# The first chunk's inverse deviations by ScalarE and VectorE instead of GpSimd, fewer warm-up matmuls, and another order of the queues

## The chip, the core and the metric

The kernel runs on one core of a Trainium2 chip. The metric is the device time of one execution in microseconds (us), as the median of several runs. The engines are TensorE (PE; its weight loads are listed as PEld), VectorE (DVE), ScalarE (ACT), GpSimd (POOL) and SyncE (SP), which here only issues transfers.

## The reference, cut to what matters

```
def _layernorm(x, axis=-1, eps=1e-5):
    return (x - mean) / jnp.sqrt(var + eps)

h  = x + A(_layernorm(x))       # x: 2048 rows of 448, bf16
h2 = h + B(_layernorm(h))
```

A is attention with 16 heads of 28: each position attends to 8 keys, at distances 0, 2, ..., 14 behind it, then the output projection wo. B is a mixer: LayerNorm, w1, gelu, a shift of four column groups along the sequence, w2, residual, then LayerNorm, w3 (448 to 1792), gelu, w4 and another residual.

## The kernel before, in words

The 2048 rows are worked in four chunks c = 0 to 3 of four 128-row tiles. For the tail the MLP regroups the tiles into five groups g = 0 to 4 (2, 4, 4, 4 and 2 tiles). Every operation is recorded once with a tag, in the functions of `_fast_path`. The tags that the text uses are:

- A1_c: statistics (`ln_stats`, L547), inverse deviation (`inv_std`, L551), normalised rows `lntm` (`normalize`, L562), and their transpose into `hT`, by TensorE and a copy out of PSUM for chunks 0 and 1, by a DMA transpose for 2 and 3
- V_c, QK_c: the projections (`phase_V` L639, `phase_QK` L685); each output is copied out of PSUM by ScalarE or VectorE (tags .e0 to .e3). `pad_wqk` (L631) spreads the weights beforehand
- S_c.g, E_c.g, AV_c.g, N_c.g: scores on TensorE, exp on ScalarE and multiplication by the mask on VectorE, values on TensorE, and the division by the softmax's sum, for half g of the heads (`phase_att`, L701). For chunks 0 and 1 the division is done block by block on VectorE (`norm_blocks`, L751). For chunks 2 and 3 the output is copied to `osb` (O), the sums travel through DRAM (Zg, Z: `zp`, `rzp`, `rz_scratch`, `rzb`; `norm_dma`, L765), and VectorE multiplies (N)
- WO_c (L789), B1_c, X_c, W1_c, G_c (L801), W2_g, B2_g (L862), L3_g, W3_g (L885), W4_g (L919): output projection, LayerNorms, w1, shifted copies, w2, w3 and w4, and the stores

At the start, four row tiles of x are loaded, two by SyncE's queue and two by ScalarE's, followed by the weights wqk and wv and the other rows of x. TensorE first runs `WARM` matmuls on a zero tile. For chunk 0, VectorE takes the statistics of two tiles, GpSimd makes the inverse deviation of both (add eps, then a power of -0.5), VectorE takes the next two, and GpSimd again. VectorE normalises all four tiles. Their transposes go to PSUM, three of the copies out of it to VectorE and one to ScalarE. Then V_0 starts.

The recorded operations are not emitted in the order of the program. `_ORDER` (L235) is a written-out list: each entry is an operation's number, with a letter where the engine is chosen there (a ScalarE, v VectorE, p GpSimd), and after the colon the PSUM banks. Each engine gets its operations in that order, and each waits for the semaphores of what it needs. `START` (L232) sets the alignment of TensorE's instruction stream. A second program for other data (L974 on) is not entered here. All instructions are emitted at L1390, so the profile tells them apart by their tiles alone.

Of the kernel before, what the change touches and what calls it, by code (L numbers as in the profile page):

```python
# [6 lines left out]
ALU = mybir.AluOpType  # L7
# [218 lines left out]
        op.clock = oc  # L226
    return plan

WARM = 18
LATE = 2  # L230

START = 158  # L232


_ORDER = """  # L235
2 1 3 4 7 8 5 6 14 12 13 0 16 15 63 62 71 17:7 76 9 10 127 20 18 21 19 26 24 22 23 27 25 28 29 30 33 34:7 31:6
36 32a 37:5 39 40:4 35v 38v 41v 72 44a 45v 47v 108 46a 11 61 102 66 106 75 105 94 100 101 109 48:60 49 50 82:42
83 84 53a 78 69 42 43a 97 110 85 56 98 129 107 135 104 133 67 131 136 130 132 134 137 138 86a 139 140 51 177 178
179 54v 59 60 87a 52:7 181 175 64 55a 180 95 57 217:24 150v 182 70 73 141v 88:60 89 176 90 91 144v 65 68 218 220
93a 151:3 183 145:2 58 147v 146a 142:5 148:4 92v 184 152v 143v 149v 74 99 198 185 186 193v 221 77 219 231:06 232  # L240
234 163:24 164 153 233 165 167a 222:76 191a 189v 103 235 166 168a 227 113p 194 228 229 114p 118p 112p 115a 117a
111p 116a 119p 196 187a 162 169:20 170 171 172 223 224 225 190 343:64 173a 96 195 174a 200 236:32 226 158:1 241
344 242 237 197 346 202 199 161a 375:2 378a 238 154:64 357:02 358 203 188 243 201 239 244 240 204 230 206 345
192 155 120p 360 205 359 361 156 159a 207 157 160a 212a 347 245:02 246 208a 247 248 249 250 251 253 257 255 254
258 252 256 259 386:46 268 387 388 270 389 214a 390a 261 362:32 391a 363 260 367 210a 368 262 269 122 121 364
271 369 379 265a 380:40 209 365 348:76 349 353 381 382 350 351 354 383 384a 385a 532:26 370 352 371:40 372 373
535 79 533 355 376a 374 216 525:26 377a 266v 211 263v 264v 267 366 81 356 526 215 528 272a 536 413:40 414 415
534 537:6 527 529 213 530:2 417 419 126 421 416 275a 418 420 538a 423 425 422 426 424 427 274v 429 428 430 531a
540 438 539 541 542 432v 273a 433v 431v 434v 276:64 277 278 436 437 279 435 280 401:02 402 403 404 281 288v 286a
292v 290v 289a 283v 287v 285v 282v 293v 291v 284v 392:46 439 406a 441v 405a 543 546 442v 393 394 545 544 395  # L250
397a 398a 400 294:02 295 296 298 297 299 302 300 303 301 306 304 305 307 309v 308v 310 125 440a 128 444:46 445
446 447 407:20 408 409 448 449 451v 460v 410 453v 456v 454a 458a 452a 457a 455v 461a 450v 459v 663:64 412a 411v
666 664 547 550 549 548 462:20 463 464 465 466 467 470 396:5 468 474 469 472 473 471 475 399a 313:26 314 315
551:04 316 80 317 552 553 555 554 556 557 559 561 558 562 123 478 476 477 479 124 563 564 560 480v 565 482v 483v
318 481a 486 574 667 567 319:62 320 321 322 324 325:04 326 327 328 566 568 323 331:62 311 312 572v 332 333 334
484 329 330 569v 571v 570v 576 665 335 573 336 670:04 337:7 443a 671 340:6 575 673 674 338 672 341 668:4 577
675:0 676v 487 580a 578a 489:62 669a 490 491 581v 485 493 678 677 582:04 583 584 586 585 587 492 679 680 681 683
684 682 488 494 598v 495:06 496 497 498 592v 599v 588v 596v 590v 594v 591v 589a 593a 595v 597v 600:24 601 602
604 603 606 607 605 608 612 610 613 609 611 614 500 615 616 617 499 501:06 502 686 503 688 505 504 507:42 508
509 685 506 511 687 510 619a 621v 339 513:7 618v 579a 626 689:40 690 514 512 620a 691 693 695 692 697 698 694  # L260
696 701 699 702 700 712 519:7 522:6 705 622 624 520 703 704 523 706 707a 521 623 633:04 634 635 636 710v 515
709v 637 708v 711 639:62 640 641 638 643 625 642 627:40 644 628 629 720:26 630 713 631 714 721 722 723 632 725
715 724 718v 645:04 730v 731 736v 732v 738v 729v 740v 737v 733a 734 728v 735a 727a 726v 739 646 647 649 719a 648
516:7 650 716v 342 517 717v 809:02 810 811 813 812 814 817 815 816 746:64 818 819 820 821 822 747 748 749 751
756 757 750 758 524 754 759 657:3 654:5 651:7 755 752 753 760 762 761 763 658 824v 660:6 823v 825 764a 741 742
743 652 659 744:7 655 766v 767v 765a 771 770 745 653 828:42 829 830 768 661 834:60 831 835 836 837 832 833
840:24 841 838 839 842 843 844 785:06 786 845 846:42 847 848 849 851 827 656 826 769 850 772 787 788 790 789
773:42 774 775 776 777 778 779:06 780 518 791:24 792 793 795 794 781 782 783 662 784 852:3 853 796 854 797:7
803:6 798 799 804 805 806:7 807 800:6 808 801 802 855:7 856 857
""".split()  # L270


def _fast_path(nc, es, flag, A_x, A_wqkv, A_wo, B_w1, B_w2, B_w3, B_w4, out):
# [15 lines left out]
    def sb(name, shape, dt):  # L289
        return es.enter_context(nc.sbuf_tensor(name, shape, dt))  # L290
# [38 lines left out]
    nmr = sb("nmr", [128, 4, NTL], F32)  # L329
    vtmp = sb("vtmp", [128, 4, NTL], F32)  # L330
    mhalf = sb("mhalf", [128, 4], F32)
    fint = sb("fint", [128, 32], I32)
    fmax = sb("fmax", [128, 1], F32)
    fbit = sb("fbit", [128, 1], BF16)
# [6 lines left out]
    def tag(name):  # L341
        S.tag = name
# [4 lines left out]
        return S.add_many("pe", calls, cost, cost + 166, mode=mode)  # L347

    def act(out_ap, in_ap, func, n, **kw):
        table = {ACT.Exp: "exp", ACT.Gelu_apprx_tanh: "gelu"}.get(func)  # L350
        lat = 186 + n / 1.2 + 93 * sum(isinstance(v, bass.AP) for v in kw.values())
        return S.add_many("act", [("activation", dict(out=out_ap, in_=in_ap, func=func, **kw))], lat - 93, lat, table=table)

# [3 lines left out]
    def dve(meth, lat, **kw):  # L357
        return S.add_many("dve", [(meth, kw)], lat - 82, lat)
# [103 lines left out]
    for c in range(1, NCH):  # L462
# [5 lines left out]
    S.add("pool", "affine_select", 300, out=ident[:], in_=ident[:], pattern=[[-1, 128]],  # L468
          compare_op=ALU.not_equal, fill=1.0, base=0, channel_multiplier=1)
    dve("memset", 62, ap=mhalf[:], constant=-0.5)  # L470
    dve("memset", 272, ap=wqk_p[:, :, :, 28:32], constant=0.0)
    pool("memset", 100, ap=hT[:, 0, :, :, 8:16], constant=0.0)
    tag("warm")
# [77 lines left out]
    def inv_std(slot, kind, i0, n, s1=1.0, s2=EPS, with_nmr=True):  # L551
        pool("tensor_scalar", 200, out=vtmp[:, slot, i0:i0 + n], in0=mv[:, kind, i0:i0 + n, 1], scalar1=s1,
             scalar2=s2, op0=ALU.mult, op1=ALU.add)
        pool("tensor_tensor", 420 + 160 * n, out=rstd[:, slot, i0:i0 + n], in0=vtmp[:, slot, i0:i0 + n],
             in1=mhalf[:, 0:n], op=ALU.pow)
        if with_nmr:
            pool("tensor_scalar", 230, out=nmr[:, slot, i0:i0 + n], in0=mv[:, kind, i0:i0 + n, 0], scalar1=-1.0,
                 scalar2=None, op0=ALU.mult)
            pool("tensor_tensor", 220, out=nmr[:, slot, i0:i0 + n], in0=nmr[:, slot, i0:i0 + n],
                 in1=rstd[:, slot, i0:i0 + n], op=ALU.mult)  # L560

    def normalize(slot, kind, i, out_ap, in_ap, dve_only=False):  # L562
        r_ = rstd[:, slot, i:i + 1]
        n_ = nmr[:, slot, i:i + 1]
        m_ = mv[:, kind, i, 0:1]
        kv = dict(out=out_ap, in0=in_ap, scalar1=m_, scalar2=r_, op0=ALU.subtract, op1=ALU.mult)
        if dve_only:
            return dve("tensor_scalar", 390, **kv)
        op = S.add_many("flex", [("tensor_scalar", dict(kv, x=n_))], 0, 0)
        op.opts = {"dve": [("tensor_scalar", kv)],  # L570
                   "act": [("activation", dict(out=out_ap, in_=in_ap, func=ACT.Identity, scale=r_, bias=n_))]}
        op.occ = {"dve": 308, "act": 652}; op.lat = {"dve": 390, "act": 745}
        return op
# [37 lines left out]
    def phase_A1(c):  # L611
        tag("A1_%d" % c)
        s = ls = c % 2
        for il in range(4):
            i = 4 * c + il
            ln_stats(0, xin[:, i, :], i)
            if c == 0 and il % 2 == 1:
                inv_std(0, 0, i - 1, 2, with_nmr=False)
        if c > 0:
            inv_std(0, 0, 4 * c, 4)  # L620
        for il in range(4):
            normalize(0, 0, 4 * c + il, lntm[:, ls, il, :, :], windows(xin[:, 4 * c + il, :]), dve_only=c == 0)
            if c in TPE:
                transpose_pe(ls, il, s)
            else:
                transpose_dma("%d_%d" % (c, il), columns(s, il), lntm[:, ls, il, :, :].rearrange("p a k -> p (a k)"), 1)
        if c > 0:
            tag("Vc_%d" % c)
            pool("tensor_copy", 215, out=hT[:, s, :, :, 8:16], in_=hT[:, 1 - s, :, :, 264:272])
# [311 lines left out]
                   op0=ALU.mult)  # L941

    phase_A1(0)
    pad_wqk()
    phase_V(0)
    init1()
# [535 lines left out]
```

## Time and profile before

| what | value |
|---|---|
| time, median of 11 runs | 194.46 us (193.89 to 195.98) |
| the profiled execution's own time | 193.9 us |
| its span in the profile | 192.1 us |
| PE busy / DVE busy / ACT busy / POOL busy | 183.7 / 128.9 / 108.3 / 43.3 us |
| granted TensorE clock in the profile | 1.00 |
| ScalarE table loads | 6, 1.28 us each |
| first matmul of V_0 | at 9.15 us |
| end of the last matmul | at 189.25 us |

The profiled execution took 1.8 us more than its span, which lies around the program. Its span is cut into 40 slices on the profile's page, each of 4.8 us, and a digit gives the busy tenths of an engine in that slice. The chain that ended last goes back from the last instruction, at each step to what released it. An idle time is put down to what ended it. A busy matmul's end is modelled, so short waits between matmuls can hide in the busy time; distances between the starts of TensorE's instructions don't have this fault.

### The profile page before, as it was taken

Reading aid. Unit: us, or ns where it says so; the run is one execution under the profiler, and the core shown is the slowest. Engines: PE = TensorE matmul, PEld = TensorE weight load, DVE = VectorE, ACT = ScalarE, POOL = GpSimd, SP = SyncE. Lnnn points to the kernel's source line nnn. Section 1 sums busy time; section 2 is a strip of 40 time slices with the busy share of each in tenths; the row PEclk is TensorE's granted clock in tenths of the full one; section 3 lists DMA queues with packets and bytes.
Section 4 is the critical chain, followed back from the end, with each engine's and each line's share of the span. In section 5 each row is a group of like instructions: output and inputs, shape, how many; then the busy total and the mean of one; then the engine's idle time right before and its main releaser. Section 6 shows DMA issues by size and latency. Waiting matters only on the chain.

```text
span 192.1 us, 6787 instructions
## 1 busy us (share of the span) xinstructions
PE 183.7 (96%) x3003; PEld 103.6 (54%) x3003; DVE 128.9 (67%) x312; ACT 108.3 (56%) x140; POOL 43.3 (23%) x107
## 2 busy tenths in 40 slices
PE   7999999998999997999989999999999999999994
PEld 2445645544666674667545454544764567554551
DVE  6899999999996967989764596960079871001221
ACT  2268789757988769859587555045670026554000
POOL 2539910408003411033800022060002300000000
DMA  5997046512096493820743700455000065000111
GB/s 151 367 284 187 19 68 76 187 31 31 6 161 112 102 231 75 266 86 3 132 95 85 170 3 0 109 78 131 0 3 0 0 135 154 3 0 13 41 51 51
DMA packets 32479, 17.77 MB, mean 93 GB/s; under 512 B 22524, under 2 KB 31932, under 8 KB 32444
## 3 DMA queue, kind: packets, MB, share of 16 engines
q1 hardware_dynamic: 32156, 17.05, 38.3%
q8 instruction: 25, 0.41, 1.0%
q10 hardware_dynamic: 288, 0.23, 0.4%
q14 instruction: 10, 0.08, 0.1%
HBM read 10.07 MB, written 1.90 MB: 62 GB/s over the span
## 4 chain that ended last, share of the span: by engine, by line
PE 76%; DVE 13%; ACT 4%; POOL 3%; DMA 1%; issue 1%
PE ps L1390 76%; DVE st L1390 3%; DVE lntm L1390 2%; DVE pt L1390 2%; DMA xin<-in_A_x_dram 1%; POOL rstd L1390 1%; DVE qk L1390 1%; ACT arena L1390 1%; POOL nmr L1390 1%; DVE xb L1390 1%; DVE xin L1390 1%; ACT pt L1390 1%; ACT qk L1390 1%; DVE hT L1390 1%; ACT vt L1390 1%
## 5 line engine op out<-in xcount | busy, mean ns | idle before, releaser
L1390 PE MATMUL ps<-actT,w_s 64*128 64x512 bf16 (+2 forms) x560 | 44.4, 313 | 0.0
L1390 PE MATMUL ps<-w_s,arena 128*128 128x448 bf16 x224 | 43.4, 353 | 0.4 <-ACT arena L1390 0.4
L1390 DVE TENSOR_TENSOR xb<-ps,xb 128x448 bf16<-128x448 f32 (+1 forms) x26 | 18.5, 725 | 33.1 <-PE ps L1390 33.1
L1390 ACT ACTIVATE arena<-ps 128x512 bf16<-128x512 f32 (+2 forms) x40 | 28.9, 766 | 17.5 <-PE ps L1390 17.4
L1390 PEld LDWEIGHTS ps<-actT,w_s 64*128 64x128 bf16 x560 | 25.9, 94 | 17.1 <-issue 0.4
L1390 PEld LDWEIGHTS ps<-w_s,arena 128*128 128x128 bf16 x224 | 21.4, 98 | 21.5 <-issue 1.0
L1390 PE MATMUL ps<-hT,arena 64*128 64x512 bf16 x224 | 25.8, 377 | 0.0
L1390 POOL TENSOR_SCALAR vtmp<-mv 128x4 f32<-128x4 f32 (+1 forms) x18 | 4.6, 254 | 85.4 <-DVE mv L1390 84.9
L1390 POOL TENSOR_TENSOR rstd<-vtmp,mhalf 128x4 f32<-128x4 f32 (+1 forms) x18 | 18.7, 1040 | 0.7
L1390 DVE BATCH_NORM_STATS2 st<-xin 128x6 f32<-128x448 bf16 x32 | 18.3, 610 | 0.9 <-DMA xin<-in_A_x_dram 0.9
L1390 PEld LDWEIGHTS ps<-hT,arena 64*128 64x128 bf16 x224 | 11.9, 94 | 10.7 <-issue 0.4
L1390 ACT ACTIVATE pt<-ps 128x1024 bf16<-128x1024 f32 x16 | 15.5, 1025 | 2.0 <-PE ps L1390 1.9
L1390 ACT ACTIVATE qk<-ps 128x1024 bf16<-128x1024 f32 x14 | 13.8, 1020 | 4.9 <-PE ps L1390 4.8
L1390 PE MATMUL ps<-arena,hT 64*64 64x448 bf16 (+1 forms) x248 | 15.3, 353 | 0.3 <-DVE hT L1390 0.3
L1390 PE MATMUL ps<-wo_s,oT 64*128 64x448 bf16 x128 | 13.1, 350 | 0.6 <-ACT vt L1390 0.6
L1390 DVE COPY gC<-gtm 32x256 bf16<-32x256 bf16 (+1 forms) x23 | 5.1, 223 | 12.5 <-ACT gtm L1390 11.9
L1390 PE MATMUL ps<-actT,w_p 64*128 64x512 bf16 (+1 forms) x140 | 13.2, 334 | 0.2 <-issue 0.2
L1390 ACT ACTIVATE lntm<-xb,nmr,rstd 128x512 bf16<-128x512 bf16 x5 | 3.9, 807 | 14.8 <-POOL nmr L1390 14.8
L1390 ACT ACTIVATE lntm<-xin,nmr,rstd 128x512 bf16<-128x512 bf16 x8 | 6.3, 817 | 8.8 <-POOL nmr L1390 8.8
L1390 PEld LDWEIGHTS ps<-actT,w_p 64*128 64x128 bf16 x140 | 8.3, 94 | 4.8 <-issue 0.6
L1390 DVE TENSOR_TENSOR pt<-pt,msk 128x1024 bf16<-128x1024 bf16 x16 | 10.4, 687 | 0.2 <-ACT pt L1390 0.2
L1390 PEld LDWEIGHTS ps<-arena,hT 64*64 64x64 bf16 (+1 forms) x248 | 7.1, 107 | 6.5 <-issue 1.2
(84 smaller groups left out, 222.8 us busy)
## 6 DMA issues: line engine op xcount, KB each, us to landing
w_s<-in_B_w_dram SPq DMA_DIRECT2D x6, 448.0 KB, 5.1
rzb<-rz_scratch SPq DMA_DIRECT2D x8, 256.0 KB, 4.6
out_dram<-xb SPq DMA_DIRECT2D x16, 112.0 KB, 1.9
xin<-in_A_x_dram SPq DMA_DIRECT2D x3, 448.0 KB, 7.0
arena<-in_A_wqkv_dram SPq DMA_DIRECT2D x2, 448.0 KB, 5.6
w_s<-in_B_w_dram SPq DMA_DIRECT2D x2, 336.0 KB, 6.5
arena<-in_A_wqkv_dram SPq DMA_DIRECT2D x2, 224.0 KB, 4.4
w_s<-in_B_w_dram SPq DMA_DIRECT2D x2, 224.0 KB, 3.3
```

The costliest lines, as they stand in the source:

```text
L1390: inst = getattr(eng, meth)(**kw)
```

## The change

- `inv_std_first` replaces GpSimd's two operations for each pair of tiles of chunk 0: ScalarE takes the square root of variance plus eps, and VectorE its reciprocal. For the first pair VectorE also makes the bias of tile 1
- tile 1 of chunk 0 is normalised by ScalarE; the other three stay on VectorE
- `WARM` goes from 18 to 14 and `START` from 158 to 128
- a one-element exp (`expd`) is recorded after A1_0; in the list of the order it stands behind the exps of E_3.0
- `_ORDER` is another list throughout. ScalarE's first table load is for the square root. A second one, for exp, stands behind the copies QK_0.e0 and QK_0.e1, in front of E_0.0's first exp; the program then loads 7 tables in all. Two of chunk 0's `hT` copies are on ScalarE and two on VectorE. The weights come in the order wv half, wqk half, wv half, wqk half
- TensorE's later order: S_0.0 stands inside QK_0.2; V_0.4 between A1_1's transposes; WO_0 behind V_1, with S_1.1 inside it and V_2.4 behind it; S_2.1 inside QK_2.0; W1_0 ahead of AV_2.0; V_3.4 and a quarter of W2_1 ahead of S_3.0; WO_2 ahead of W3_0.00; the last quarter of W2_2 behind W3_1.12; and the w3 and w4 blocks of the tail in another order
- choices of engine: in X_0, X_1, X_2 and X_3 eight `xb` tiles move from ScalarE to VectorE; small G copies move the other way; O_2.0 is copied by VectorE

```diff
-WARM = 18
+WARM = 14
 LATE = 2
-START = 158
+START = 128
...
 _ORDER = """
-2 1 3 4 7 8 5 6 14 12 13 0 16 15 63 62 71 17:7 76 9 10 127 20 18 21 19 26 24 22 23 27 25 28 29 30 33 34:7 31:6
+2 1 4 3 7 6 8 5 12 17 0 16 13 15 45 65 74 64 67 68 79 21 19 18:7 22 20 28 23 24 25 26 29 27 35 30 32 36:7 33:6
...
+    epsb = sb("epsb", [128, 1], F32)
+    expd = sb("expd", [128, 1], F32)
...
+    dve("memset", 62, ap=epsb[:], constant=EPS)
...
+    def inv_std_first(i0):
+
+        v, r_, m_ = (t[:, 0, i0:i0 + 2] for t in (vtmp, rstd, mv))
+        act(v, m_[:, :, 1], ACT.Sqrt, 2, bias=epsb[:])
+        dve("reciprocal", 160, out=r_, in_=v)
+        if i0 == 0:
+            dve("scalar_tensor_tensor", 150, out=nmr[:, 0, 1:2], in0=mv[:, 0, 1, 0:1], scalar=-1.0, in1=rstd[:, 0, 1:2],
+                op0=ALU.mult, op1=ALU.mult)
...
             ln_stats(0, xin[:, i, :], i)
             if c == 0 and il % 2 == 1:
-                inv_std(0, 0, i - 1, 2, with_nmr=False)
+                inv_std_first(i - 1)
...
-            normalize(0, 0, 4 * c + il, lntm[:, ls, il, :, :], windows(xin[:, 4 * c + il, :]), dve_only=c == 0)
+            if c == 0 and il == 1:
+                act(lntm[:, ls, 1, :, :], windows(xin[:, 1, :]), ACT.Identity, 512, scale=rstd[:, 0, 1:2], bias=nmr[:, 0, 1:2])
+            else:
+                normalize(0, 0, 4 * c + il, lntm[:, ls, il, :, :], windows(xin[:, 4 * c + il, :]), dve_only=c == 0)
...
     phase_A1(0)
+    tag("exp")
+    act(expd[:], epsb[:], ACT.Exp, 1)
     pad_wqk()
```

## The prediction, made before the changed kernel was run

> **What bounds the kernel now.** I read the page first, for each engine's load and where it lies.
>
> ```profile
> span 192.1 us, 6787 instructions
> ...
> PE   7999999998999997999989999999999999999994
> ...
> DVE  6899999999996967989764596960079871001221
> ACT  2268789757988769859587555045670026554000
> ```
>
> TensorE is at nine tenths nearly everywhere. VectorE is full in the first ten slices (to 48 us), half free from 100 us. So the change can only gain in three ways: an earlier V_0, less waiting by TensorE, a shorter tail. The tail is alike in both kernels (one W4 tile, one addition, one store). What TensorE waited for is the second view:
>
> ```profile
> PE ps L1390 <- DVE oT L1390: 1.4, 1, 1.4
> PE ps L1390 <- DVE qk L1390: 1.1, 1, 1.1
> PE ps L1390 <- DVE pt L1390: 0.7, 2, 0.6
> PE ps L1390 <- ACT vt L1390: 0.6, 1, 0.6
> PE ps L1390 <- DVE zp L1390: 0.5, 1, 0.5
> PE ps L1390 <- ACT arena L1390: 0.4, 1, 0.4
> PE ps L1390 <- DVE hT L1390: 0.3, 1, 0.3
> ```
>
> The first is the wait at the start; all the others come to 4.0 us with the two small lines left out here (0.2 each). That is the whole stock of waits that another order can win back. By the timeline they lie at 9.15 (V_0), 21.22 (S_0.1), 24.73 (AV_0.0), 48.02 (S_2.1), 53.10 (WO_1), 59.71 (W1_0), 76.83 (W2_1), 96.79 (AV_3.1) and 114.36 (W4_1.0). Third, the chain that ended last, for the stretch that the change is about:
>
> ```profile
> 5.94 0.23 DVE mv L1390 x2
> 6.16 0.08 issue
> 6.24 0.27 POOL vtmp L1390
> 6.51 0.07 issue
> 6.58 0.76 POOL rstd L1390
> 7.34 0.02 issue
> 7.37 0.99 DVE lntm L1390 x2
> 8.35 0.75 DVE hT L1390 x2
> 9.11 0.04 issue
> 9.15 10.23 PE ps L1390 x194
> ```
>
> Between the last statistics (6.16) and the last normalised tiles stand 1.2 us of GpSimd. The 18 warm-ups end near 7.8, where the first transposes start, so they too would hold an earlier start.
>
> **Step 1, the start.** VectorE's first pair of aggregates ends at 4.90. ScalarE's root starts about 0.07 later and takes 0.19 to 0.28 (nearest row: 128x64 without a bias operand, 0.24); I take 0.25, so 5.22. VectorE is then inside the third statistics (to 5.39). The reciprocal of 128x2 takes some 0.15 (rows: 128x16 0.236, 128x64 0.553, 6.6 ns an element), the bias operation 0.15 (row: the 128x1 fbit, 0.156), each with a semaphore's 0.05: 5.75. Fourth statistics to 6.3, aggregates 6.55, tile 0 normalised 6.9. ScalarE normalises tile 1 from 5.8 for 0.82 (its lntm row) to 6.6, and only then takes the second root: 6.9. Reciprocal 7.1, tiles 2 and 3 at 0.39 each: 7.9, against 8.36. Two hT copies on each engine instead of three and one: VectorE ends near 8.7. V_0 starts at 8.7 instead of 9.15: a gain of 0.45. Its wv now lands third of four weight pieces; the third landed at 7.96, which hides it with 0.7 us to spare. The mask, wv_2 and w1_p memsets moved ahead of x end near 3.3, before x lands (3.51): nothing. A pad waits for the last piece (9.14), VectorE's cover to QK_0 being 2 us: nothing. If root or reciprocal cost twice as much, the gain is 0.2; if cheaper, 0.6.
>
> **Step 2, the second table load.** ScalarE must load exp behind QK_0.e1.
>
> ```profile
> 76.70 1.28 ACT L1390 ACT_TABLE_LOAD   x1
> 78.00 1.94 ACT L1390 ACTIVATE pt<-ps 128x1024 bf16<-128x1024 f32 x2
> ```
>
> The row says a switch costs 1.30 to the next exp. The Trainium skill, ScalarE: Activation LUTs, section "What ACT_TABLE_LOAD costs", says 1283 ns and 1380 ns of drain, and its rule is to do all of one set first: it speaks against the change. With the row: QK_0 ends at 14.5, e0 and e1 (1.02 each) at 15.95, the load to 17.25, S_0.0 ends at 16.95, so E_0.0 begins at 17.3 instead of 17.15. Queued behind it on ScalarE stand two exps (2.05), an hT copy (0.6) and QK_0.e2 (1.02), for which S_0.1 waits: about 21.05, against 21.22. So of the 0.45 only 0.15 is left there. With the page's 2.66, S_0.1 would start at 22.4. I take the row.
>
> **Step 3, VectorE's stretch to 53 us.** It has less to do before the masks: a normalised tile and two hT copies moved to ScalarE (3 x 0.4), and a vt copy of 1.09 swapped for one of half the size. N_0.0 and N_0.1 are four chains of 0.65 + 0.22 + 0.62 + 0.65, that is 8.6; they start when AV_0.0 ends (25.1), and no statistics lie between them any more: 33.9. WO_0 at 34.05. In before it starts at 36.59, behind S_1.1 and V_2.4 (1.64): 34.95. A gain of 0.9. It is spent again. ScalarE's queue to QK_2.e3 holds four normalised A1_3 tiles (0.81 each), E_1.1 and two copies, and ends at 45.5: S_2.1 at 45.6, against 48.02 less 2.2 for the QK_2.0 work that now follows: 0.2 left. N_1's last transpose ends near 52.9 by the same sum, WO_1 at 53.0 against 53.10. I carry a gain of **0.1** through here; between -0.9 and +1.
>
> **Step 4, the new order from 53 us.** W2_1 waits 1.06 for a PSUM bank from QK_3.e2. Now V_3.4 (0.88) and a quarter of W2_1 come first and the copy is on VectorE's clear stretch: I take 0.9 saved. But WO_2 now stands ahead of W3_0.00 and needs N_2's four products (2.5) behind two L3_0 tiles: 0.3 lost. AV_3.1 waits for the mask of E_3.1, behind the same three B1_2 tiles: as before. W4_1.0 waits 0.37 for the last W3_1 copy; a quarter of W2_2 (0.57) now covers it, after a neighbouring copy is paid: 0.3 saved. In the tail L3_3's transposes landed 0.3 before W3_3 needed them; the new order gives 13.5 us from W2_3's end instead of 15.4, but needs only about 13, since its normalising no longer waits for W4_2's additions: nothing. Sum: **0.9** saved; the X tiles moved to VectorE (8 x 0.39) lie where it waits for PE: nothing, and 0.4 each in front of W2_0 if it doesn't.
>
> **Step 5, small costs.** Where TensorE changes between kinds of tiles (full, quartered, attention) the start of the next block comes about 0.1 later (a quad of 0.65 lasts 0.74 before scores). There are 46 such changes instead of 42: **0.4** lost, between 0 and 0.4. The alignment has no row; the 0.23 put down to issue at 59.71 is the nearest, so -0.2 to +0.2, taken as zero. The expd behind E_3.0 costs one short ScalarE operation while it waits: nothing.
>
> **The sum.** 0.1 + 0.9 - 0.4 = 0.6 to 0.7 us off the profiled execution's 193.9 (192.1 and 1.8 around it). I take 0.7: 193.2 by the profile. The median of the runs is 0.56 above that execution, so **193.7**.
>
> **Rivals.** *Swallowed.* VectorE and ScalarE set the pace to 60 us, and each bound above met the old time within 0.2. If the W2_1 wait only moves to WO_2, everything returns: 194.4. For it: steps 2 and 3 show it twice. Against it: the 1.06 has a clear cause, removed.
>
> *The sums' round trip gets late (slower).* AV_2.0 now follows W1_0 (3.0 us), so its copy O_2.0 and Zg_2.0 go out near 62.1 instead of 59.55; Zg_2.0 stands on SP behind two weight loads, and the rz store behind B1_1's transposes, which need ScalarE's lntm behind gA, gtm and three gC. The reciprocal waits at VectorE's head, with a gB copy, V_3.e1, four X_0 tiles and W2_0's additions queued behind it, and QK_3 and W2_0 wait for those. In before rzb landed from 69.8 to 73.67. I make it 0.6 later, 74.3; from 77 on every us is a us on WO_2, now moved forward. At 2.5 us late the cost is 1.2 at WO_2 and 0.7 through W2_0: 195.6.
>
> *The clock isn't granted in time (slower).* The weight loads stand 0.427 apart until 6.45 and 0.216 after: the clock doubled 5.1 us after TensorE's first matmul. The Trainium skill, TensorE: Matmul & The Clock Gate, section "Part 1: The HAM clock gate", wants one busy window of 3.4 us whose phase varies, so the doubling could come up to 6.8 us after, and 14 slow warm-ups fill 6.0. By the row 14 end at 6.9, already fast, and free the transposes. By the page about a quarter of executions would run V_0 and part of QK_0 at half speed: 3.4 us of slow work, 1.2 to 1.7 lost. As the median this would be 195.7.
>
> **Chances.** Forecast 0.50, swallowed 0.15, round trip or another wait like it in the reshuffled stretch 0.23, clock 0.12. So faster 0.50, same 0.15, slower 0.35; 0.3% (0.6 us) is about what a measurement of this kernel can tell from no change. The likeliest case alone spans 192.3 to 194.0: step 3 giving its 0.9, or nothing. The range reaches to the slow cases' middle: 192.3 to 195.9.
>
> **What would show it.** V_0 starting near 8.7; one load of 1.28 between QK_0.e1 and E_0.0, S_0.1 not before 21; WO_0 about 34 and WO_1 about 53; the wait at W2_1 gone and at most 0.3 at WO_2; the last matmul ending near 188.5. Wrong would be: warm loads still 0.427 apart when V_0 runs, rzb of chunk 2 landing behind 77, or a new wait above 0.6 anywhere between 25 and 115 us.

## The result, and the profile after

| | before | changed |
|---|---|---|
| median of the runs | 194.44 us (50 runs, 193.59 to 196.66) | 192.99 us (13 runs, 192.29 to 194.17) |
| the profiled execution, its span | 193.9, 192.1 us | 192.94, 191.2 us |
| ratio to before | | 0.9918, 95% interval 0.9897 to 0.9939 |

The changed kernel is 0.8% faster. The forecast was 193.7. By the medians the gain is 1.45 us, about twice what was forecast. By the profiled executions it is 0.96 where 0.7 was forecast; the rest of the difference is the 0.56 between the median and the profiled execution of before, which I had carried over. After, the median stands only 0.05 above it.

The head of the page of the changed kernel, with the rows of the 40 slices:

```profile
span 191.2 us, 6790 instructions
...
PE   7899999999888998999999999999999999999994
...
ACT  2859899598858949938658930117691326554000
```

TensorE is as full as it was, and its last slices are the same. ScalarE's slice from 4.8 to 9.6 us went from 2 tenths to 8: it has taken work of the first chunk. What TensorE waited for, from the changed kernel's waits (us in total, times, longest):

```profile
PE ps L1407 <- DVE oT L1407: 1.3, 1, 1.3
PE ps L1407 <- ACT qk L1407: 0.8, 2, 0.5
PE ps L1407 <- DMA hT<-lntm: 0.6, 1, 0.6
PE ps L1407 <- DVE mhalf L1407: 0.6, 1, 0.6
PE ps L1407 <- DMA actT<-lntm: 0.6, 1, 0.6
PE ps L1407 <- ACT vt L1407: 0.5, 1, 0.5
PE ps L1407 <- ACT gC L1407: 0.3, 1, 0.3
PE ps L1407 <- DVE lntm L1407: 0.3, 1, 0.3
```

The waits for a mask (DVE pt), for the sums (DVE zp), for W3's copy (ACT arena) and half of the one at W2_1 are gone. Two waits for transfers are new, 1.2 us together. The chain that ended last, from 5.7 to 21 us:

```profile
5.73 0.81 ACT lntm L1407
7.01 0.42 DVE lntm L1407
...
7.91 0.76 DVE hT L1407 x2
8.77 5.34 PE ps L1407 x78
14.14 1.94 ACT qk L1407 x2
16.10 1.28 ACT L1407
17.39 1.94 ACT pt L1407 x2
19.33 0.49 ACT hT L1407
19.82 0.93 ACT qk L1407
20.88 15.76 PE ps L1407 x464
```

The 1.2 us of GpSimd are gone from it, and the unnamed 1.28 at 16.10 is the second table load.

Starts of TensorE's instructions at points where both kernels have the same work behind them show where the gain was made and lost:

| at | before | changed | gain so far |
|---|---|---|---|
| V_0 | 9.15 | 8.77 | 0.38 |
| S_0.1 | 21.22 | 20.88 | 0.34 |
| AV_0.0 | 24.73 | 24.32 | 0.41 |
| WO_1 | 53.10 | 52.50 | 0.60 |
| QK_3.0 | 61.45 | 61.59 | -0.14 |
| S_3.1 | 89.18 | 88.86 | 0.32 |
| end of AV_3.1 (start of W3_1) | 97.53 | 96.71 | 0.82 |
| W4_1.0 | 114.36 | 113.09 | 1.27 |
| end of the last matmul | 189.25 | 188.37 | 0.88 |

So everything won up to 53 us is lost again between 53 and 61.5, and the lasting gain comes from 71 to 115 us. TensorE's lines at three of those places in before (W2_1, AV_3.1, W4_1.0):

```profile
76.83 0.56 PE L1390 MATMUL ps<-w_s,gA 64*128 64x448 bf16 x4 [1.06 <-DVE qk L1390]
96.79 0.81 PE L1390 MATMUL ps<-pt,vt 64*32 64x52 bf16 x80 [0.55 <-DVE pt L1390]
114.36 2.82 PE L1390 MATMUL ps<-w_s,arena 128*128 128x448 bf16 x14 [0.37 <-ACT arena L1390]
```

and in changed, for the last two:

```profile
95.14 1.64 PE L1407 MATMUL ps<-pt,vt 64*32 64x52 bf16 x160
113.09 3.20 PE L1407 MATMUL ps<-w_s,arena 128*128 128x448 bf16 x16
```

The three steps repeat in the profiles of the experiments below. Ten profiles have the changed order in this stretch, and three the old one:

| from, to | old order | changed order |
|---|---|---|
| QK_3.2, S_3.1 | 17.28 to 17.36 | 16.98 to 17.01 |
| S_3.1, W3_1 | 8.34 to 8.35 | 7.85 to 7.88 |
| W3_1, W4_1.0 | 16.83 to 16.84 | 16.37 to 16.38 |

What differs from profile to profile of the changed order lies ahead of QK_3.2.

### The profile page after: what moved, and what is told of

Same layout as the page of the kernel before. It is cut to its first block, busy times and chain, and to the rows that moved or that the text cites. A ratio compares the mean times of both kernels' runs of the same rounds, so it can differ in the third digit from the quotient of the medians.

```text
span 191.2 us, 6790 instructions
## 1 busy us (share of the span) xinstructions
PE 183.0 (96%) x2999; PEld 102.6 (54%) x2999; DVE 128.6 (67%) x313; ACT 112.2 (59%) x149; POOL 41.4 (22%) x101
## 4 chain that ended last, share of the span: by engine, by line
PE 72%; DVE 11%; ACT 9%; DMA 4%; SPq 2%; issue 1%
PE ps L1407 72%; DMA hT<-lntm 3%; ACT qk L1407 2%; ACT pt L1407 2%; DVE st L1407 2%; ACT gC L1407 2%; SPq L1407 2%; DVE rzb L1407 2%; DMA xin<-in_A_x_dram 1%; DVE oT L1407 1%; DVE osb L1407 1%; DVE xin L1407 1%; DVE pt L1407 1%; ACT gtm L1407 1%; DVE lntm L1407 1%
## 5 line engine op out<-in xcount | busy, mean ns | idle before, releaser
L1407 PEld LDWEIGHTS ps<-actT,w_s 64*128 64x128 bf16 x560 | 26.4, 94 | 16.9 <-DVE xb L1407 0.4
L1407 POOL TENSOR_TENSOR rstd<-vtmp,mhalf 128x4 f32<-128x4 f32 (+1 forms) x16 | 18.1, 1131 | 1.1
L1407 PEld LDWEIGHTS ps<-hT,arena 64*128 64x128 bf16 x224 | 10.7, 94 | 12.6 <-ACT qk L1407 0.8
L1407 ACT ACTIVATE lntm<-xin,nmr,rstd 128x512 bf16<-128x512 bf16 x13 | 10.2, 807 | 9.0 <-POOL nmr L1407 8.3
L1407 POOL TENSOR_SCALAR nmr<-mv 128x4 f32<-128x4 f32 (+1 forms) x16 | 4.0, 251 | 42.6 <-DVE mv L1407 42.4
L1407 DVE COPY gC<-gtm 32x256 bf16<-32x256 bf16 (+1 forms) x15 | 3.3, 220 | 13.6 <-ACT gtm L1407 13.2
L1407 PEld LDWEIGHTS ps<-arena,hT 64*64 64x64 bf16 (+1 forms) x248 | 7.6, 107 | 5.9 <-ACT gC L1407 0.8
```

The costliest lines, as they stand in the source:

```text
L1407: inst = getattr(eng, meth)(**kw)
```

## The experiments

All were run in five rounds beside the kernel before, in four sets. Its median was 194.68, 194.21, 194.67 and 194.85 us in the four, so kernels of different sets are compared by their ratios to it; changed has 0.9918. "Changed" is the changed kernel.

### The number of warm-ups

old_warm14 is the kernel before with one line changed, new_warm18 the changed kernel with the reverse.

```diff
-WARM = 18
+WARM = 14
```

> The kernel before with WARM 14 alone. Theory (the statistics and GpSimd's powers set V_0, the warm-ups only hold the first transposes): V_0 stays at 9.1 to 9.2 us, and the time within 0.3 us of before. Rival (18 warm-ups hold the start in the executions where the clock is granted late, and that is why the median of before lies 0.5 us above its profiled execution): the time falls by 0.4 us or more and the spread of the runs shrinks. Second rival (14 are too few for the clock): weight loads of V_0 still 0.2 us or more apart, time up by 1 us or more.

Measured: 194.77 us, ratio 1.0019 [0.9986, 1.0052]; V_0 at 9.07. Fewer warm-ups alone bring nothing that these runs can tell.

> The changed kernel with WARM 18 alone. Theory: the warm-ups end about 0.9 us later (four at 0.216), the first transposes wait for them, and V_0, set by the last hT copies, comes 0.2 to 0.4 us later; of that 0.2 at most reaches the end, 193.0 to 193.3 us. Rival (the four fewer warm-ups carry the gain of the medians): 193.6 us or more.

Measured: 193.39 us, ratio 0.9923 [0.9889, 0.9957]; V_0 at 9.45, later than expected: the last warm-ups ended at 7.8, and everything behind them followed. So 18 warm-ups can hold the start. Whether they do depends on when the distance between their weight loads halves: at 6.8 us here, but at 5.2 in old_root below, where the first transposes wait for a normalised tile instead.

In this profile V_0 starts 0.30 later than in the kernel before, and yet the three steps of the table above take what they take in changed; and the ratio is changed's within the noise. The lasting gain does not hang on the start.

In no profile does V_0 run at half speed: its 56 matmuls take 2.84 us in changed and in each of its ten variants, as long as V_1's do later in changed, and the first 44 take 2.28 in before, old_root and old_warm14. The distance between warm-up loads halved between 3.9 and 6.8 us in all profiles but one. In new_early_exp all 14 loads were still 0.43 apart, the last at 6.42, and the first transposes began at 7.06 instead of 6.59 to 6.74. So a late clock can hold the start by some 0.4 us, but it didn't touch V_0's own speed. The 13 runs of changed (192.29 to 194.17) also show no quarter of executions that lose 1.2 us or more, as that rival had it.

### Root and reciprocal without the new order, and the new order without them

old_root is the kernel before, its order kept, with ScalarE's root and VectorE's reciprocal for chunk 0 (the edit is shortened here; it also adds the `epsb` tile and the name of the root's table):

```diff
-                inv_std(0, 0, i - 1, 2, with_nmr=False)
+                v = vtmp[:, 0, i - 1:i + 1]
+                act(v, mv[:, 0, i - 1:i + 1, 1], ACT.Sqrt, 2, bias=epsb[:])
+                dve("reciprocal", 160, out=rstd[:, 0, i - 1:i + 1], in_=v)
```

> The kernel before with ScalarE's root and VectorE's reciprocal in the first chunk, same order, 18 warm-ups, all four tiles on VectorE. Theory (the start alone is given back at S_0.1 through the exp table's load and VectorE's queue): V_0 at 8.8 to 9.0 us, a second table load of 1.28 us in front of E_0.0, time 194.2 to 194.6 us, that is within 0.3 of before. Rival (the start carries through): 193.7 us or less.

Measured: 194.44 us, ratio 0.9995 [0.9968, 1.0022]. V_0 starts at 8.86 and S_0.1 at 20.93, so 0.3 is won, and AV_0.0 starts at 24.75 as ever. The timeline of old_root shows why (start, duration, engine, operation; the idle time before it in brackets):

```profile
23.25 2.00 DVE L1393 TENSOR_TENSOR pt<-pt,msk 128x1024 bf16<-128x1024 bf16 x3
24.75 0.80 PE L1393 MATMUL ps<-pt,vt 64*32 64x52 bf16 x80 [0.52 <-DVE pt L1393]
```

In before the same wait was 0.15. VectorE reaches the masks no earlier (23.25, and 23.23 in before), so TensorE waits for them instead. What takes up the 0.3 is one normalised tile ahead of the masks, which lasts twice as long as in before. In old_root, then in before:

```profile
22.18 1.15 DVE L1393 TENSOR_SCALAR lntm<-xin,mv,rstd 128x512 bf16<-128x512 bf16 x1
```

```profile
22.72 0.59 DVE L1390 TENSOR_SCALAR lntm<-xin,mv,rstd 128x512 bf16<-128x512 bf16 x1
```

In both it ends at 23.3, and in both GpSimd's six copies into `w_p`, which begin at 20.86 and 20.84, end at 23.4. In old_warm14 the tile takes 1.14 and ends at 23.5, the copies at 23.6. Whether the copies hold VectorE there was not tried.

new_pow is changed with GpSimd's two operations back in chunk 0. What else the change does, tile 1 on ScalarE included, stays:

```diff
-        act(v, m_[:, :, 1], ACT.Sqrt, 2, bias=epsb[:])
-        dve("reciprocal", 160, out=r_, in_=v)
+        pool("tensor_scalar", 200, out=v, in0=m_[:, :, 1], scalar1=1.0, scalar2=EPS, op0=ALU.mult, op1=ALU.add)
+        pool("tensor_tensor", 740, out=r_, in0=v, in1=mhalf[:, 0:2], op=ALU.pow)
```

> The changed kernel with GpSimd's add and power in the first chunk in place of ScalarE's root and VectorE's reciprocal, its mhalf constant made first and tile 1's bias behind the fourth statistics; order otherwise as in the changed kernel. No table load in front of E_0.0. Theory (the order of the queues carries most of the gain): V_0 0.3 to 0.5 us later (9.1 to 9.3), E_0.0 waits for no table, S_0.1 within 0.3 us of the changed kernel's 20.9, time 193.0 to 193.4 us. Rival (the root's earlier start carries the gain through): 193.7 us or more.

Measured: 193.02 us, ratio 0.9902 [0.9868, 0.9936]: all of the gain within the noise, without the operation that the change is named for. V_0 starts at 8.82, not at the 9.1 to 9.3 that I expected. Two reasons show in its timeline:

```profile
7.35 0.15 POOL L1407 MEMSET qk<- 128x64 bf16 x1
...
7.44 0.73 DVE L1407 TENSOR_SCALAR lntm<-xin,mv,rstd 128x512 bf16<-128x512 bf16 x2 [0.87 <-POOL rstd L1407]
...
8.34 0.83 DVE L1407 COPY hT<-ps 128x512 bf16<-128x512 bf16 x2 [0.17 <-PE ps L1407]
```

VectorE has two hT copies to make instead of three. And its last two normalised tiles take 0.73. In before they took 0.99, beside a long GpSimd operation:

```profile
7.30 0.59 POOL L1390 TENSOR_SCALAR_AFFINE_SELECT rzb<-rzb 128x408 bf16<-128x408 bf16 x1
7.37 0.99 DVE L1390 TENSOR_SCALAR lntm<-xin,mv,rstd 128x512 bf16<-128x512 bf16 x2 [0.59 <-POOL rstd L1390]
```

That the neighbour caused the 0.26 was not tried by itself.

### The second table load

new_early_exp is changed with the one-element exp behind ScalarE's wv copy, where ScalarE has nothing to do:

```diff
- 49a 46a 78 
+ 49a 46a 44 78 
...
- 475 559 44 320 
+ 475 559 320 
```

> The changed kernel with the one-element exp put behind ScalarE's wv copy, where ScalarE idles 1.27 us, so that the exp table is loaded there. Theory (the second load delays E_0.0 by less than 0.1 us, since ScalarE would wait for S_0.0 anyway): E_0.0 at 17.3, S_0.1 within 0.15 us of 20.9, time within 0.2 us of 193.0. Rival (the load is what gives the early start back): S_0.1 0.3 us earlier and 192.7 us or less.

Measured: 192.71 us, ratio 0.9924 [0.9908, 0.9941], which doesn't tell it from changed. ScalarE's timeline:

```profile
10.86 1.28 ACT L1407 ACT_TABLE_LOAD   x1
...
17.41 1.94 ACT L1407 ACTIVATE pt<-ps 128x1024 bf16<-128x1024 f32 x2 [1.23 <-PE ps L1407]
```

With the load out of the way ScalarE waits 1.23 for S_0.0 instead, and the first exp starts at 17.41, against 17.39 with the load in front and 17.35 in new_pow, which needs none. These three start V_0 at 8.88, 8.77 and 8.82, so the distance from V_0 says more: to S_0.1 it is 12.10 to 12.11 in all six profiles with the load in front of E_0.0, and 12.02 in all five without it. The load of 1.28 lies in a gap of nearly the same size, and costs 0.09.

### Alignment

```diff
-START = 128
+START = 158
```

> The changed kernel with START 158, as the kernel before had it. Theory (the alignment has no part in the gain beyond 0.2 us): no wait put down to issue above 0.3 us in the profile, time within 0.3 us of the changed kernel's 193.0. Rival (the alignment keeps waits for instructions away): one or more waits of TensorE put down to issue of 0.5 us or more, as the 18-warm-up version shows 0.81 and 0.60, and 193.5 us or more.

Measured: 193.09 us, ratio 0.994 [0.9924, 0.9955]. Two waits put down to issue, 0.21 each. The intervals of this ratio and of changed's overlap, so no part of the gain is shown to be alignment; a few tenths of a us are not excluded.

### The cover at W2_1

new_v34late puts V_3.4 behind W2_1 again; the rest of the order stays.

```diff
-312v 399:7 311v 402a 552 465:24 551 666:60 313 550 466 467 553 667 469 669 468 470 473
+312v 552 465:24 311v 551 666:60 313 550 466 467 553 667 469 669 468 399:7 402a 470 473
```

> The changed kernel with V_3.4 moved back behind W2_1, so that nothing covers the copies QK_3.e2 and QK_3.e3. Theory (the cover is worth what it lasts): TensorE idles 1.3 to 1.5 us behind QK_3.2 instead of 0.6, AV_3.1 comes 0.6 to 0.9 us later than 95.98, time 193.5 to 193.9 us. Rival (swallowed by VectorE's queue in front of AV_3.1, where the changed kernel already waits): AV_3.1 within 0.3 us, time within 0.3 us of 193.0.

Measured: 194.51 us, ratio 1.0002 [0.9978, 1.0026]: moving eight matmuls of 0.88 us in all gives the whole gain back, more than I expected. TensorE's timeline there, new_v34late first:

```profile
76.60 0.55 PE L1407 MATMUL ps<-w_s,gA 64*128 64x448 bf16 x4 [1.40 <-ACT qk L1407]
...
80.22 0.57 PE L1407 MATMUL ps<-arena,hT 128*64 128x448 bf16 x4
...
81.81 2.44 PE L1407 MATMUL ps<-wo_s,oT 64*128 64x448 bf16 x24 [0.64 <-ACT vt L1407]
```

and changed:

```profile
74.99 0.57 PE L1407 MATMUL ps<-arena,hT 128*64 128x448 bf16 x4
...
76.47 0.55 PE L1407 MATMUL ps<-w_s,gA 64*128 64x448 bf16 x4 [0.53 <-ACT qk L1407]
...
80.22 2.44 PE L1407 MATMUL ps<-wo_s,oT 64*128 64x448 bf16 x24
```

W2_1 starts at almost the same time in both (76.60 and 76.47), because it waits for a copy on ScalarE that doesn't move. Whether 0.88 us of work stands in front of it or behind it is 0.88 us of waiting. On top of that WO_2 now waits 0.64 for the copy of V_3.4's output. ScalarE is free for it (it idles 0.91 before), but V_3.4's matmuls now stand directly in front of WO_2, and nothing covers the copy. WO_2 is 1.59 later than in changed, AV_3.1 too (97.57 against 95.98). The run shows what the cover at W2_1 carries; the parts at AV_3.1 and W4_1.0 were not taken back one by one.

### The new wait at QK_3.0

The chain of changed, just ahead of QK_3.0 (start, duration, what):

```profile
56.30 5.20 DMA hT<-lntm
61.50 0.09 issue
61.59 9.82 PE ps L1407 x134
```

and SyncE's own timeline there (SPq is SyncE's queue):

```profile
51.63 1.60 SPq L1407 DMA_TRANSPOSE actT<-lntm  x1
53.27 2.35 SPq L1407 DMA_TRANSPOSE hT<-lntm  x1
55.67 0.58 SPq L1407 DMA_DIRECT2D w_s<-in_B_w_dram  x1
56.30 1.19 SPq L1407 DMA_TRANSPOSE hT<-lntm  x1
```

Two hT transposes of A1_3 stand behind B1_0's actT transpose, which cannot be issued before its rows are ready (51.63), and one of them behind a weight load too. The last lands at 61.50, and QK_3.0 needs it. new_transposes_first moves the two ahead:

```diff
-216 532 126 420 421 403
+532 126 420 421 403
...
-430 432 212 541a 543
+430 432 541a 543
...
-218 263 392 394a
+218 216 212 263 392 394a
```

> The changed kernel with the two late DMA transposes of chunk 3 (for hT) moved on SyncE's queue from behind B1_0's transpose to in front of the w3 and w4 loads. Theory (QK_3.0 waits 0.6 us because these wait in the queue behind B1_0's transpose, whose rows are ready only at 51.6): the transposes land before 56, QK_3.0 starts 0.5 to 0.7 us earlier than 61.59, and 0.3 to 0.6 us of that reaches the end: 192.4 to 192.7 us. Rival (something else ends at the same time, or the loads behind are late for W3_0): 192.9 us or more.

Measured: 192.40 us, ratio 0.9912 [0.9894, 0.993]. SyncE's timeline now:

```profile
42.52 5.77 SPq L1407 DMA_TRANSPOSE hT<-lntm  x3
48.34 1.09 SPq L1407 DMA_DIRECT2D w_s<-in_B_w_dram  x2
51.12 3.35 SPq L1407 DMA_TRANSPOSE actT<-lntm  x1
```

QK_3.0 starts at 60.67 instead of 61.59, and the 0.6 for hT is gone from the waits; 0.9 now stands at W1_0 for actT. Not all of the 0.92 is the move's: in this profile WO_1 already starts 0.70 earlier. From AV_2.1's start to QK_3.0's it is 0.91 instead of 1.45, so the wait that went was worth 0.54 here. In best_pow, below, the same move brings QK_3.0 only from 61.56 to 61.38, since W1_0 then waits 0.87 for actT. The profiled execution took 192.24, against 192.94, but by the ratios (0.9912 and 0.9918) this kernel is not shown to be faster than changed.

### What the root is worth once nothing swallows it

best_pow is new_pow with the same move; best_early_exp is new_early_exp with it.

> The changed kernel with chunk 0's inverse deviations on GpSimd again (as in new_pow) and the two transposes of A1_3 issued ahead of B1_0's (as in new_transposes_first). My theory: the two edits touch different places and add up. Root and reciprocal carry nothing of the gain, so this kernel takes what new_transposes_first takes, 192.2 to 192.6 (ratio 0.989 to 0.992 of before), with QK_3.0 near 60.7 and no table load ahead of E_0.0. Rival: the root is worth its 0.3 at V_0 once the wait at QK_3.0 no longer swallows it; then this kernel is 0.3 to 0.4 later than new_transposes_first, near 192.8.

> The changed kernel with the two transposes of A1_3 issued ahead of B1_0's, and the one-element exp moved up to ScalarE's wv copy, so that the second table load lies near 10.9 where ScalarE has nothing to do. My theory: the load in front of E_0.0 costs nothing (0.04 by new_pow), so this is new_transposes_first again: 192.2 to 192.6. Rival: with the wait at QK_3.0 gone, the load's 1.28 in front of E_0.0 becomes visible: 0.3 or more faster than new_transposes_first, 192.0 or less.

Measured: best_pow 192.64 us, ratio 0.9885 [0.985, 0.992]; best_early_exp 192.01 us, ratio 0.9874 [0.9821, 0.9926]. QK_3.0 at 61.38 and 60.61. Both fall between what my theory and the rival gave them, and the intervals overlap: neither is settled by the times. But V_0 starts at 8.82 and 8.54 in the two, and these starts have a cause that can be read.

### What V_0 waited for

Kernels with the very same start show V_0 at 8.45 or at 8.8. In the timeline of changed:

```profile
7.91 0.76 DVE L1407 COPY hT<-ps 128x512 bf16<-128x512 bf16 x2 [0.17 <-PE ps L1407]
8.62 0.06 DVE L1407 MEMSET mhalf<- 128x4 f32 x1
8.77 0.76 PE L1407 MATMUL ps<-arena,hT 64*64 64x448 bf16 x12 [0.58 <-DVE mhalf L1407]
```

and of new_transposes_first, whose order is the same up to there:

```profile
7.91 0.76 DVE L1407 COPY hT<-ps 128x512 bf16<-128x512 bf16 x2 [0.17 <-PE ps L1407]
8.45 1.33 PE L1407 MATMUL ps<-arena,hT 64*64 64x448 bf16 x24 [0.26 <-DVE hT L1407]
```

VectorE is equal to the hundredth, so the label "DVE mhalf" in the first cannot be right: V_0 doesn't read that tile. The second half of wv had landed (issue and time to landing, from the view of transfers) at 8.53 in changed and at 8.21 in new_transposes_first. In new_early_exp it landed at 8.63, and there V_0 starts at 8.88 (hT was 0.2 later too) with the right label, DMA arena<-in_A_wqkv_dram. The distance is 0.24 and 0.25. wv_first and best_wv_first have the two halves of wv ahead of wqk, in changed and in best_early_exp:

```diff
-2 1 4 3 7 6 8 5 12
+2 1 4 3 7 8 6 5 12
```

> The changed kernel with both halves of wv loaded ahead of both halves of wqk (the kernel before had them so: wv, wv, then wqk). In the changed kernel's own profile V_0 started at 8.77, 0.24 after the second half of wv had landed (8.53), though hT was ready; in other executions with the same start it landed by 8.21 and V_0 started at 8.45. My theory: the landing of that half holds V_0 in some executions. With it loaded second it lands near 7.5 to 7.9 and V_0 starts at 8.45 to 8.55 always; QK_0 needs the pads of wqk, which then end near 10.4, a little ahead of QK_0.0's 11.2. S_0.1 near 20.55. The wait at QK_3.0 swallows most of it: 192.7 to 193.0. Rival: V_0's start varies for another reason and stays at 8.8, or the later wqk holds QK_0 by more: 193.2 or more.

> best_early_exp with both halves of wv ahead of both halves of wqk. My theory: the profile of best_early_exp already had wv in time (V_0 at 8.54), so only the executions in which it was late gain: 191.8 to 192.1, V_0 at 8.45 to 8.55. Rival: wqk's later landing holds QK_0.0 (beyond 11.3): 192.3 or more.

Measured: wv_first 192.81 us, ratio 0.9881 [0.9832, 0.9931], V_0 at 8.40, QK_0.0 at 11.18, S_0.1 at 20.50; best_wv_first 192.41 us, ratio 0.9864 [0.9814, 0.9914], V_0 at 8.43. wv landed at 6.89 and 7.02. The theory's starts are met, and wqk holds nothing up (QK_0.0 at 11.20 in best_wv_first). The time of best_wv_first is the one that the rival gave, without its cause; with 6 runs each this stays open. The intervals of all these kernels overlap with changed's, 0.9897 to 0.9939: none of them is shown to be faster than it, or than another of them.

With wv in time, root and reciprocal start V_0 at 8.40 to 8.54 (six profiles), GpSimd at 8.82 (two). So they are worth 0.3 to 0.4 at V_0, and "the root carries nothing", which I drew from new_pow, was too strong: changed's own profile happened to have wv late.

## Why the prediction was right, and where it was not

**Step 1** (V_0 at 8.7, wv hidden with 0.7 to spare). The time was right and a reason was wrong. VectorE ended at 8.67 as forecast (8.7), but V_0's first matmuls need only the first of its two hT copies, which ended at 8.34: V_0 could start at 8.45. And the cover for wv was taken from one landing in before. In the changed order it landed between 7.84 and 8.63, and held V_0 in two of the six profiles that have that order, the root and 14 warm-ups. The start gained 0.38 and 0.27 in these two, 0.6 to 0.7 in the other four.

**Step 2** (one load, 0.15 left at S_0.1). The first exp was forecast at 17.3 and started at 17.39. The load was measured at 1.28 and 17.39 - 16.10 = 1.29 to the next exp; by the Trainium skill's figures (ScalarE: Activation LUTs, section "What ACT_TABLE_LOAD costs") it would have been 2.66. That page's rule to do all of one set first (section "Table sets: the hidden batching unit") speaks against the change; the switch that it warns of cost 0.09 at S_0.1. S_0.1 gained 0.34 instead of 0.15: I had summed single durations (2.05 + 0.6 + 1.02), and in the chain the four operations take 1.94 + 0.49 + 0.93, since neighbours overlap.

**Step 3** (0.1 carried). WO_0 at 34.18 (forecast 34.05), S_2.1 at 45.09 (45.6), WO_1 at 52.50 (53.0): the course was right, S_2.1 half a microsecond earlier (25.1 and 8.6 are 33.7, not 33.9, as I had it on the way to WO_0). The failure is behind it: between 53 and 61.5 the changed kernel loses 0.74, and no step of mine had that. There are two new waits for transfers, 0.57 at W1_0 and 0.64 at QK_3.0, against one of 0.23 in before. I had followed who waits for ScalarE and VectorE, and SyncE's queue only for the sums' round trip. The hT transposes stand in the same queue, one actT transpose further back. By the measure that I set myself, a new wait above 0.6 between 25 and 115, the 0.64 at QK_3.0 is a miss.

**Step 4** (0.9). From QK_3.0 to W4_1.0 it was 1.41. The parts: 0.36 of 0.6 between QK_3.2 and S_3.1, since the wait at W2_1 went from 1.06 to 0.53 and not to nothing. Its copy is on ScalarE, behind gA, gtm and five gC, and not on VectorE as I wrote. WO_2, which I charged 0.3, has no wait. AV_3.1, for which I said "as before", lost its wait of 0.55. ScalarE takes one of the normalised tiles there, so VectorE has three instead of four; and VectorE makes two masks instead of one before those tiles, so one fewer stands behind them. Its last masks end at 95.92 instead of 96.74. At W4_1.0 0.45 instead of 0.3.

**Step 5** (0.4 lost). From W4_1.0 to the end 0.4 is lost against before's profile, but 0.32 of it is one wait, at W2_4 for a gC copy. A cost of mode changes was neither shown nor excluded.

The tail was not the "nothing" of step 4 in every execution. In the old order the last transpose of L3_3 landed 0.27 and 0.13 us before W3_3 needed it in before and in old_root, and in old_warm14 it landed too late:

```profile
162.16 11.62 PE L1390 MATMUL ps<-actT,w_s 64*128 64x512 bf16 x140 [0.65 <-DMA actT<-lntm]
```

No profile of the changed order has a wait there. How many executions of the kernel before had it is not on record, so whether it is part of why the medians gained 1.45 and the profiles 0.96 stays open.

The sum came out near because its errors offset: 0.5 more to 53 us, 0.74 less to 61.5, 0.5 more to 115. That is luck. What was right in the mechanism is step 4's main term, the cover at W2_1.

**The rivals.** *Swallowed*: true of the start (old_root; and in changed to QK_3.0), false of W2_1 (new_v34late). *Round trip late*: rzb of chunk 2 landed until 75.33, later than my 74.3 but before 77, and no wait for it shows at WO_2. *Clock*: V_0 at half speed in none of the profiles, the transposes held by it in new_early_exp. Its own loss of 1.2 to 1.7 on 193.7 makes 194.9 to 195.4, not 195.7.

## What to carry to other kernels

An early start is worth what the next full engine or queue lets through. Compare both kernels at points of equal work, and the place where the gain goes is seen at once. When an order is rewritten, follow each queue that issues transfers too: a transfer that is ready waits behind one that isn't. A transfer's landing is a range, not a number, so ask how far the cover reaches in the worst execution.

## What the runs showed of the hardware

- A table load in front of ScalarE's first exp cost 0.09 us of the 1.28 that it takes, because ScalarE would have waited 1.23 there anyway. In front of the load stood 0.02 of idle time, and the exp began 0.01 behind it.
- TensorE's waits put down to issue, inside runs of small matmuls, differ from kernel to kernel and are not tied to the place of a change: none in changed, 0.76 in old_root at 60.19, 0.84 in new_v34late at 47.08, 1.10 in new_early_exp at 61.81. They can make a profile unlike the median: new_early_exp's profiled execution took 193.5 with a median of 192.71. In new_v34late they were taken up before QK_3.0 (61.60 against 61.59 in changed). What causes them was not found; with START at 158 instead of 128 there were two of 0.21 in place of none.
- Two DMA transposes whose rows were ready stood in SyncE's queue behind one whose rows were not (issued at 51.63), and landed at 57.41 and 61.50; ahead of it they landed at 48.92 and 49.46.
- The distance between warm-up loads halved 2.5 to 5.5 us after TensorE's first matmul in thirteen profiles, and in one not within the 5.1 us that its warm-up loads lasted.
- The same load of weights landed up to 0.8 us earlier or later in kernels whose queue is the same up to there (7.84 to 8.63).
